# Block-sparse attention then token mix: the weight decoding kept out of the last two attention units, the first two mix steps' x turned earlier, and the block tables built after the first scores

## The chip, the cores and the metric

The kernel runs on one core of one Trainium2 chip. The metric is the device time of one launch in microseconds; a lower number is better. The engines are called as in the profile: PE is TensorE (PEld its weight loads), DVE VectorE, ACT ScalarE, POOL GpSimd, SP SyncE, whose queue issues nearly all DMAs.

## The reference

Two stages. The attention output of all heads is the token mix's input x. Everything is float32; the inputs of the mix weights are float64 words that the kernel decodes itself.

```python
def _attn_ref(q, k, v, sampled_blocks):            # B=4, H=8, S=768, D=64
    scores = scale * np.matmul(q, k.transpose(0, 1, 3, 2))
    # kept: blocks of 32 with |i - j| <= 1, first and last block row and column,
    # and 3 sampled key blocks for each query block
    scores = np.where(mask, scores, -1000000000.0)
    attn = np.exp(scores - np.max(scores, axis=-1, keepdims=True))
    attn = attn / (np.sum(attn, axis=-1, keepdims=True) + 1e-09)
    return np.matmul(attn, v)

def _moe_ref(x, w_theta, w_tok_r, w_tok_i, w_ch):  # x: 4 x 768 x 512
    theta = x @ w_theta
    zr, zi = x * np.cos(theta), x * np.sin(theta)
    y = np.einsum('ts,bsd->btd', w_tok_r, zr) + np.einsum('ts,bsd->btd', w_tok_i, zi)
    u = x + y
    return u + np.maximum(u @ w_ch, 0.0)
```

## The kernel before

**Attention** works on 52 units: for each of two pairs of batches, four wide units (the first and last query block against all 768 keys) and then 22 narrow units i = 1 to 22, one query block each. A unit passes through these steps: POOL copies the key blocks it needs into `kg` (L259) and gathers its sampled value rows into `vb` by an indirect DMA (L281); PE makes the scores `S` (L298, wide L386); DVE takes their extremes `m` (L301, wide L392); ACT takes exponentials into `P` (L310, wide L400); PE turns `P` into `T` (L316), and ACT copies that to `pT` (L318); PE multiplies by the values into `X` (L350) for two units at a time; DVE normalises into `xo` (L331 to L335), and SP writes `xo` to the DRAM buffer `xs` (L369). The steps of neighbouring units are interleaved by hand: the loop over n (L471 to L541) does the scores of unit n+1, the weights of n+1, the transposition of n, the values of earlier units, and the gathers of n+2. This stands in a `manual_schedule` block.

**Decoding.** The weights of theta and of the token mix are 22 pieces of 64-bit words. A piece takes a load by SP (L61, 512 KB), then three phases: `bits` (DVE L69 to L71, after ACT's `start` L65), `rest` (DVE L77, L79) and `low` (DVE L85, L86, after ACT's `high` L82). These 66 phases are dealt out over the units by `shares`: weight 0 for the first two units, 2 for a wide one, 1 for any other (L432 to L436). The loop gives each unit the phases that bring it up to its share: `decoder.ahead` does ACT's part, `decoder.go` DVE's part, and the low phase of a piece issues the load of the piece after next.

**Tables.** `Tables` loads the sampled block numbers and turns them into the row numbers that POOL's gathers use. `make` (L130 to L161) is nine small DVE operations on `sb_scratch` and `sb_block` and some on POOL; `rest` follows in unit 0.

**Token mix.** `follow` is a generator, resumed three times. Before its first `yield` it issues the loads of x for mix steps 0 and 1 from `xs`: `xr` (L585) for the transposed form, `xa` (L572) for the plain one, four DMAs each, in a pool whose room is that of the key tile `kb`, so it can begin when POOL's last copy from `kb` is done. Then it does `turn(0)` and `turn(1)` (DVE transposes to `r` L601, ACT's high part `xTh` L602, DVE's low part `xTl` L603; `r` has one buffer), loads ACT's Sin table (L689), and does `theta(0)` and `theta(1)` (PE L611 to L613, then a chain of ACT L615, L616 and DVE L618 to L620, ACT L622 to L624). `turned` multiplies by x and splits (L633 to L637), and `mix` (L649 to L651) accumulates `y` on PE, 24 matmuls for each of 48 steps. The four PSUM banks of `y` are those of attention's `T` and `X`, so the first `mix` waits for the last `xo`. At the end `out` multiplies by the channel weights (L672 to L674).

Before the change the loads of x are issued at the start of the unit before the last, and everything from `turn(0)` to `theta(1)` in the last unit, behind its transposition and its decoding (L533 to L535).

Of the kernel before, what the change touches and what calls it, by code (L numbers as in the profile page):

```python
# [88 lines left out]
class Decoder:  # L89
# [11 lines left out]
    def ahead(self, n):  # L101

        for k in range(self.at, min(self.at + n, 3 * len(self.pieces))):
            piece = self.pieces[k // 3]
            if k % 3 == 0:
                piece.start()
            elif k % 3 == 2:
                piece.high()

    def go(self, n):  # L110
        for k in range(self.at, min(self.at + n, 3 * len(self.pieces))):
            piece = self.pieces[k // 3]
            (piece.bits, piece.rest, piece.low)[k % 3]()
            if k % 3 == 2 and k // 3 + 2 < len(self.pieces):
                self.pieces[k // 3 + 2].load(self.pool, self.queue)
        self.at += n
# [64 lines left out]
def attention(tc, qT, qE, kT, vr, sampled, xs, ident, pieces, follow):  # L181
# [8 lines left out]
    nc = tc.nc  # L190
    with ExitStack() as ctx, ExitStack() as scored, ExitStack() as early:
# [8 lines left out]
        cp = ctx.enter_context(tc.tile_pool(name="acp", bufs=1))  # L200
# [30 lines left out]
        def load_k(bp, b, pp):  # L231
            if (b, pp) == (0, 0):
                kbs[bp] = kp.tile([P, 8, NB, 32], F32, tag="kb", name=f"kb{bp}")
            nc.sync.dma_start(kbs[bp][:, 4 * b + 2 * pp : 4 * b + 2 * pp + 2], kT[bp, b][:, 2 * pp : 2 * pp + 2])
# [5 lines left out]
        def load_edges(bp):  # L240
            qes[bp] = ep.tile([P, 2, 4, 64], F32, tag="qe", name=f"qe{bp}")
            nc.sync.dma_start(qes[bp].rearrange("r b p f -> r (b p f)"), qE[bp])

        def turn_edges(bp):
            t = qes[bp].rearrange("r b p f -> r (b p f)")
            nc.vector.tensor_scalar(t, t, -0.125, None, op0=ALU.mult)
# [126 lines left out]
        def load_v_wide(bp, b, pp):  # L373
            v = vp.tile([P, 6, 260], F32, tag="vw", name=f"vw{bp}_{b}_{pp}")
            c0 = 260 * (2 * b + pp)
            nc.sync.dma_start(v, vr[768 * bp : 768 * bp + 768, c0 : c0 + 260].rearrange("(c s) f -> s c f", s=P))
            vws[bp, b, pp] = v
# [51 lines left out]
        units = []  # L429
# [1 line left out]
            units += [(bp, "w", x) for x in WIDE] + [(bp, i, None) for i in range(1, NB - 1)]  # L431
        shares, total = [], 0.0  # L432
        for n in range(len(units)):
            weight = 0.0 if n < 2 else 2.0 if units[n][1] == "w" else 1.0
            total += weight
            shares.append(total)  # L436

        def do(n, inner, wide=None):

            if 0 <= n < len(units):  # L440
                bp, i, x = units[n]
                if i != "w":
                    inner(bp, i)
                elif wide:
                    wide(bp, *x)

        def is_wide(n):
            return 0 <= n < len(units) and units[n][1] == "w"

        def first_of_pair(n):  # L450
            return n < len(units) and units[n][1] == "w" and units[n][2] == (0, 0)
# [3 lines left out]
        with tc.manual_schedule():  # L455
            load_edges(0)
            load_k(0, 0, 0)
            tab = Tables(nc, wp, sampled)
            turn_edges(0)
            tab.make(nc, cp)  # L460
            load_k(0, 0, 1)
            load_v_wide(0, 0, 0)
            load_k(0, 1, 0)
            load_v_wide(0, 0, 1)
            load_k(0, 1, 1)
            for i in (1, 3):
                load_q(0, i)
            decoder = Decoder(pieces, stage, nc.sync)
            do(0, scores, scores_wide)
            do(0, weights, weights_wide)  # L470
            for n in range(len(units) + 1):  # L471
                if n == len(units) - 2:
                    early.close()
                    next(follow)
                phases = 0
                if n < len(units):
                    phases = round(shares[n] / total * 3 * len(pieces)) - decoder.at
                if n + 4 < len(units) and not is_wide(n + 4) and units[n + 4][:2] not in ((0, 1), (0, 3)):
                    load_q(*units[n + 4][:2])
                if first_of_pair(n + 10):  # L480
                    load_edges(1)
                for pp in range(2):
                    if first_of_pair(n + 16 - 6 * pp):
                        load_v_wide(1, 0, pp)
                do(n + 2, gather_k)
                if first_of_pair(n + 3):
                    for b, pp in WIDE:
                        load_k(1, b, pp)
                do(n + 3, number_blocks)
                do(n + 2, scale_q)  # L490
                if first_of_pair(n + 2):
                    turn_edges(1)
                decoder.ahead(phases)
                last = None
                if is_wide(n):
                    bp, _, x = units[n]
                    if n and not is_wide(n - 1):
                        last = units[n - 2][:2]
                        values(*last)
                    turn_wide(bp, *x, 0)  # L500
                    do(n + 1, scores, scores_wide)
                    if n and is_wide(n - 1):
                        values_wide(bp, *units[n - 1][2], 1)
                    do(n + 1, weights, weights_wide)
                    turn_wide(bp, *x, 1)
                    decoder.go(phases)
                    if n == 0:
                        tab.rest(nc)
                    if last:
                        finish(*last)  # L510
                    values_wide(bp, *x, 0)
                    if n and is_wide(n - 1):
                        finish_wide(bp, *units[n - 1][2])
                elif n == len(units):
                    last = units[n - 2][:2]
                    values(*last)
                    finish(*last)
                else:
                    bp, i, _ = units[n]
                    do(n + 1, scores, scores_wide)  # L520
                    if i == 1:
                        values_wide(bp, *units[n - 1][2], 1)
                    elif i % 2:
                        last = bp, i - 2
                        values(*last)
                    if i % 2:
                        do(n + 1, weights, weights_wide)
                        turn(bp, i)
                    else:
                        turn(bp, i)  # L530
                        do(n + 1, weights, weights_wide)
                    decoder.go(phases)
                    if n == len(units) - 1:  # L533
                        scored.close()
                        next(follow)  # L535
                    if last:
                        finish(*last)
                    if i == 1:
                        finish_wide(bp, *units[n - 1][2])
                do(n + 2, load_pair)  # L540
                do(n + 2, gather_v)  # L541
            assert not decoder.left(), decoder.left()


def token_mix(tc, w, ch_pieces, xs, outT, bias, nb):
# [7 lines left out]
    nc = tc.nc  # L553
    with ExitStack() as late, ExitStack() as ctx:
# [3 lines left out]
        half_pi, up_int, down_int, early = bias  # L558
# [3 lines left out]
        def at(k):  # L562
            return k // 12, (k // 6) % 2, k % 6
# [23 lines left out]
        def tok(b, j):  # L587
            return [t[:, :, 128 * (j % 3) : 128 * (j % 3) + 128] for t in xT[b, j // 3]]

        def turn(k):  # L590
            b, h, j = at(k)
            if h:
                return
            if j % 3 == 0:
                tp = tps[min((2 * b + j // 3) % 3, 1)]
                xT[b, j // 3] = [tp.tile([P, 4, 384], F32R, tag=f"xT{x}", name=f"xT{x}{b}_{j}") for x in "hl"]
            hi, lo = tok(b, j)
            raw = xr.pop((b, j))
            r = xp.tile([P, 4, 128], F32, tag="r", name=f"r{k}", bufs=1)
            for c in range(4):  # L600
                nc.vector.transpose(r[:, c, :].rearrange("p (i t) -> p i t", t=32), raw[:, :, c])  # L601
            nc.scalar.copy(hi, r)  # L602
            nc.vector.tensor_tensor(lo, r, hi.bitcast(F32), op=ALU.subtract)  # L603
# [77 lines left out]
        for k in range(2):  # L681
            load_raw(k, xp)
            load(k)
        yield
        ps_h = ctx.enter_context(tc.tile_pool(name="ps_h", bufs=3, space=PSUM, side="right"))
        ps_o = ctx.enter_context(tc.tile_pool(name="ps_o", bufs=1, space=PSUM, side="right"))
        turn(0)
        turn(1)
        nc.scalar.activation(early, half_pi, AF.Sin)  # L689
        theta(0)  # L690
        theta(1)
# [4 lines left out]
        cp = late.enter_context(tc.tile_pool(name="mcp", bufs=1))  # L696
# [117 lines left out]
```

## Time and profile before

| what | us |
|---|---|
| median of 3 runs | 617.61 (616.85 to 617.62) |
| the profiled execution's own time | 614.82 |
| span of its instructions | 613.0 |
| PE busy | 546.7 (89%) |
| DVE busy | 451.7 (74%) |
| ACT busy | 334.7 (55%) |
| POOL busy | 150.1 (24%) |

The span is counted from the first instruction to the last, and 1.8 us of the execution lie around it. All times of rows are microseconds from the start of the span, so a row tells at which place of the program it stands: attention runs to about 274 us, the token mix from there to the end. The columns of a timeline row are start, duration, engine, line, operation, destination<-sources, shapes, count, and in brackets how long the engine had been idle before it and what ended that. The columns of a windows row are the stretch, its length, then busy time and number of instructions of PE, PEld, DVE, ACT and POOL, the granted PE clock as a share of full speed, the DMA engines' busy share and GB/s.

### The profile page before, as it was taken

What the parts mean: (1) busy time and instruction counts of PE and PEld (TensorE: products, weight loads), DVE (VectorE), ACT (ScalarE), POOL (GpSimd) and SP (SyncE); (2) the same over time, 40 slices, a digit from 0 to 9 for tenths busy, and PEclk for the clock granted to TensorE, in tenths of its full rate; (3) what the DMA queues carried; (4) which work ended last, traced back from release to release, by engine and by line L of the source; (5) the groups of instructions that cost most, each with busy time, mean ns of one, the idle gap of its engine ahead of it and who ended that gap; (6) DMA issues with size and microseconds to landing.
All of it is one profiled execution on the core that took longest, in us unless ns stands there. A gap on an engine that the chain in (4) does not pass through costs nothing.

```text
span 613.0 us, 16813 instructions
## 1 busy us (share of the span) xinstructions
PE 546.7 (89%) x6636; PEld 482.5 (79%) x6636; DVE 451.7 (74%) x1063; ACT 334.7 (55%) x708; POOL 150.1 (24%) x262
## 2 busy tenths in 40 slices
PE   4869787866788898869999999999999999999997
PEld 1546565553565575559999999999999999999997
DVE  2798898854988989768999894846974748657554
ACT  2567767653665776655756563455542655433520
POOL 1457877604166888300000000000000000000000
PEclk9999999887998999878999999999999999999999
DMA  8788999785588988835531242211342111211002
GB/s 293 272 239 241 323 310 324 227 307 167 165 258 275 287 254 275 218 107 163 151 113 57 66 137 83 74 46 40 105 121 74 48 52 47 79 61 57 18 1 103
DMA packets 62686, 95.59 MB, mean 156 GB/s; under 512 B 9104, under 2 KB 44560, under 8 KB 62608
## 3 DMA queue, kind: packets, MB, share of 16 engines
q1 hardware_dynamic: 56272, 71.09, 38.3%
q0 software_dynamic: 6336, 23.43, 11.8%
q8 instruction: 52, 0.85, 0.6%
q14 instruction: 26, 0.21, 0.1%
HBM read 81.90 MB, written 12.58 MB: 154 GB/s over the span
## 4 chain that ended last, share of the span: by engine, by line
PE 66%; DVE 13%; ACT 8%; DMA 7%; issue 3%; SPq 2%; POOL 0%; POOLq 0%; DVEq 0%; ACTq 0%
PE y L649 9%; PE y L650 9%; PE y L651 9%; PE X L350 5%; PE S L298 4%; PE T L316 4%; PE o L674 4%; PE o L673 4%; PE o L672 4%; PE h L613 3%; PE h L612 3%; PE h L611 3%; DVE m L301 3%; ACT pT L318 2%; ACT P L310 2%
## 5 line engine op out<-in xcount | busy, mean ns | idle before, releaser
L259 POOL COPY kg<-kb 128x256 f32 (+2 forms) x202 | 103.3, 550 | 64.1 <-PE S L298 32.7
L310 ACT ACTIVATE P<-S,m 128x256 f32<-128x256 f32 x176 | 69.1, 479 | 30.1 <-DVE m L301 25.5
L649 PE MATMUL y<-w_tok_r_hi,zh 128*128 128x384 f32 x192 | 65.3, 340 | 4.0 <-DVE xo L335 3.7
L301 DVE TENSOR_REDUCE m<-S 128x2 f32<-128x512 f32 x88 | 56.3, 681 | 12.3 <-PE S L298 12.0
L650 PE MATMUL y<-w_tok_r_lo,zh 128*128 128x384 f32 x192 | 64.9, 338 | 0.0
L651 PE MATMUL y<-w_tok_r_hi,zl 128*128 128x384 f32 x192 | 64.9, 338 | 0.0
L649 PE MATMUL y<-w_tok_i_hi,zh 128*128 128x384 f32 x192 | 64.9, 338 | 0.0
L650 PE MATMUL y<-w_tok_i_lo,zh 128*128 128x384 f32 x192 | 64.8, 338 | 0.0
L316 PEld LDWEIGHTS T<-ident,P 128*128 128x128 f32 x352 | 39.6, 146 | 30.9 <-ACT pT L318 22.7
L316 PE MATMUL T<-ident,P 128*128 128x128 f32 x352 | 50.4, 288 | 14.7 <-ACT pT L318 13.5
L318 ACT COPY pT<-T 128x1024 f32<-128x1024 f32 x44 | 44.8, 1018 | 33.1 <-PE T L316 32.9
L651 PE MATMUL y<-w_tok_i_hi,zl 128*128 128x384 f32 x192 | 62.3, 338 | 0.0
L298 PE MATMUL S<-kg,q 64*32 64x256 f32 x1408 | 54.5, 406 | 7.0 <-issue 6.1
L611 PE MATMUL h<-w_theta_hi,xTh 128*128 128x256 f32 x192 | 54.7, 285 | 2.4 <-ACT xTh L602 2.4
L615 ACT ACTIVATE t<-h,up_int 128x256 f32<-128x256 f32 x48 | 22.8, 474 | 60.4 <-PE h L613 56.5
L613 PE MATMUL h<-w_theta_hi,xTl 128*128 128x256 f32 x192 | 54.6, 285 | 0.0
L612 PE MATMUL h<-w_theta_lo,xTh 128*128 128x256 f32 x192 | 54.4, 284 | 0.0
L281 POOL DMA_INDIRECT vb<-in_vr_dram,rows x44 | 44.9, 1019 | 35.6 <-PE X L350 28.4
L673 PE MATMUL o<-ul,w_ch_hi 128*128 128x384 f32 x128 | 42.9, 335 | 0.0
L674 PE MATMUL o<-uh,w_ch_lo 128*128 128x384 f32 x128 | 42.9, 335 | 0.0
L672 PE MATMUL o<-uh,w_ch_hi 128*128 128x384 f32 x128 | 42.4, 335 | 0.0
L649 PEld LDWEIGHTS y<-w_tok_r_hi,zh 128*128 128x128 f32 x192 | 36.7, 191 | 4.5 <-ACT cs L623 3.9
(129 smaller groups left out, 1248.8 us busy)
## 6 DMA issues: line engine op xcount, KB each, us to landing
xa<-xs SPq DMA_DIRECT2D x192, 64.0 KB, 2.0
vw<-in_vr_dram SPq DMA_DIRECT2D x8, 780.0 KB
kb<-in_kT_dram SPq DMA_DIRECT2D x8, 768.0 KB
xr<-xs SPq DMA_DIRECT2D x96, 64.0 KB, 2.0
out_dram<-of SPq DMA_DIRECT2D x32, 192.0 KB, 1.9
va<-in_vr_dram SPq DMA_DIRECT2D x22, 260.0 KB, 6.1
q<-in_qT_dram SPq DMA_DIRECT2D x22, 256.0 KB, 6.2
xs<-xo SPq DMA_DIRECT2D x88, 64.0 KB, 5.2
```

Source lines behind the costliest of these rows:

```text
L259: nc.gpsimd.tensor_copy(dst, blocks.rearrange("r g s f -> r s g f"))
L298: nc.tensor.matmul(sc[32 * p : 32 * p + 32, e, b, :], q[rows, b, p, :], keys[rows, :, :, place(b, p), :], start=True, stop=True)
L301: nc.vector.tensor_reduce(m[:, e], sc[:, e], axis=AX.X, op=ALU.min)
L310: nc.scalar.activation(pt[:, e, b, :], sc[:, e, b, :], AF.Exp, bias=m[:, e, b : b + 1], scale=-1.0)
L316: nc.tensor.transpose(t[:, k, :], pt, ident)
L611: nc.tensor.matmul(ps, hi[:, c, :], wh[:, c, :], start=c == 0, stop=False)
L612: nc.tensor.matmul(ps, hi[:, c, :], wl[:, c, :], start=False, stop=False)
L613: nc.tensor.matmul(ps, lo[:, c, :], wh[:, c, :], start=False, stop=c == 3)
L649: nc.tensor.matmul(acc, zh[:, dd], wh[:, j, tt], start=j == 0 and m == 0, stop=False)
L650: nc.tensor.matmul(acc, zh[:, dd], wl[:, j, tt], start=False, stop=False)
L651: nc.tensor.matmul(acc, zl[:, dd], wh[:, j, tt], start=False, stop=j == 5 and m == 1)
L673: nc.tensor.matmul(ps, wh[:, c, :], ul, start=False, stop=False)
```

## The change

There are four parts. The last two units get decoding weight 0, so the 66 phases are dealt out over a total weight of 54 instead of 56, and where a unit holds the first and third phase of one piece, `high` is issued between them. The loads of x for steps 0 and 1 are written at the end of the third unit from the end, behind POOL's last copy from `kb`. `turn(0)` and `turn(1)` stand in the last unit but one, and a new `yield` keeps the table load and the two theta steps back for the last unit, behind its transposition. `tab.make` is called after the first wide scores instead of before them.

```diff
@@ Decoder
-            elif k % 3 == 2:
+            elif k % 3 == 2 and k - 2 < self.at:
                 piece.high()
     def go(self, n):
             piece = self.pieces[k // 3]
+            if k % 3 == 2 and k - 2 >= self.at:
+                piece.high()
             (piece.bits, piece.rest, piece.low)[k % 3]()
@@ attention
-            weight = 0.0 if n < 2 else 2.0 if units[n][1] == "w" else 1.0
+            weight = 0.0 if n < 2 or n >= len(units) - 2 else 2.0 if units[n][1] == "w" else 1.0
...
             turn_edges(0)
-            tab.make(nc, cp)
             load_k(0, 0, 1)
...
             do(0, scores, scores_wide)
+            tab.make(nc, cp)
             do(0, weights, weights_wide)
             for n in range(len(units) + 1):
-                if n == len(units) - 2:
-                    early.close()
-                    next(follow)
...
                 do(n + 2, gather_k)
+                if n == len(units) - 3:
+                    early.close()
+                    next(follow)
...
                     decoder.go(phases)
-                    if n == len(units) - 1:
+                    if n == len(units) - 2:
+                        next(follow)
+                    elif n == len(units) - 1:
                         scored.close()
                         next(follow)
@@ token_mix
         yield
+        turn(0)
+        turn(1)
+        yield
         ps_h = ctx.enter_context(tc.tile_pool(name="ps_h", bufs=3, space=PSUM, side="right"))
         ps_o = ctx.enter_context(tc.tile_pool(name="ps_o", bufs=1, space=PSUM, side="right"))
-        turn(0)
-        turn(1)
         nc.scalar.activation(early, half_pi, AF.Sin)
```

Where this moves instructions is seen in the order of each engine's queue. The numbers behind names are those of buffers, and lines of the changed kernel stand two to five lower. First DVE at the start of the program, before the change:

```order
L246 TENSOR_SCALAR qe_126<-qe_126 128x512
L134 CAST sb_scratch<-sb_scratch 128x72
L136 TENSOR_SCALAR sb_scratch<-sb_scratch 128x72
L138 CAST sb_block<-sb_scratch 1x3x24
L155 TENSOR_TENSOR sb_scratch<-sb_scratch 128x72
...
L160 SCALAR_TENSOR_TENSOR sb_scratch<-sb_scratch 128x72
L392 TENSOR_REDUCE mw_00_179<-SW_000_169 128x1
L392 TENSOR_REDUCE mw_00_179<-SW_001_170 128x1
L392 TENSOR_REDUCE mw_01_204<-SW_010_194 128x1
```

And the same place after it:

```order
L248 TENSOR_SCALAR qe_126<-qe_126 128x512
L394 TENSOR_REDUCE mw_00_158<-SW_000_148 128x1
L394 TENSOR_REDUCE mw_00_158<-SW_001_149 128x1
L136 CAST sb_scratch<-sb_scratch 128x72
L138 TENSOR_SCALAR sb_scratch<-sb_scratch 128x72
L140 CAST sb_block<-sb_scratch 1x3x24
L157 TENSOR_TENSOR sb_scratch<-sb_scratch 128x72
...
L162 SCALAR_TENSOR_TENSOR sb_scratch<-sb_scratch 128x72
L394 TENSOR_REDUCE mw_01_204<-SW_010_194 128x1
```

The two reductions of the first wide unit now stand ahead of the nine table operations, and these stand ahead of the second unit's reductions.

Second, DVE at the end of attention, from the last narrow unit's reduction (`m_22`) on, before the change:

```order
L69 TENSOR_SCALAR da_tok_i_4274<-da_tok_i_4274 128x512
L70 TENSOR_SCALAR da_tok_i_4274<-da_tok_i_4274 128x512
L71 SCALAR_TENSOR_TENSOR da_tok_i_4274<-raw_tok_i_4091,da_tok_i_4274 128x512
L301 TENSOR_REDUCE m_22_4365<-S_22_4348 128x2 x2
L77 TENSOR_SCALAR ds_tok_i_4434<-da_tok_i_4274 128x512
L79 SCALAR_TENSOR_TENSOR raw_tok_i_4091<-raw_tok_i_4091,ds_tok_i_4434 128x512
...
L335 TENSOR_TENSOR xo_19_4440<-X_19_4368,sm_19_4437 128x512
L85 TENSOR_TENSOR da_tok_i_4274<-da_tok_i_4274,w_tok_i_hi 128x512
L86 TENSOR_TENSOR w_tok_i_lo<-da_tok_i_4274,raw_tok_i_4091 128x512
L601 STREAM_TRANSPOSE r_4468<-xr_0_4328 128x128 x4
L603 TENSOR_TENSOR xTl_0_4467<-r_4468,xTh_0_4466 128x4x128
```

And after it:

```order
L85 TENSOR_TENSOR da_tok_i_4124<-da_tok_i_4124,w_tok_i_hi 128x512
L86 TENSOR_TENSOR w_tok_i_lo<-da_tok_i_4124,raw_tok_i_3932 128x512
L303 TENSOR_REDUCE m_22_4371<-S_22_4354 128x2 x2
L605 STREAM_TRANSPOSE r_4442<-xr_0_4295 128x128 x4
L607 TENSOR_TENSOR xTl_0_4441<-r_4442,xTh_0_4440 128x4x128
L605 STREAM_TRANSPOSE r_4449<-xr_1_4305 128x128 x4
L607 TENSOR_TENSOR xTl_0_4441<-r_4449,xTh_0_4440 128x4x128
...
L337 TENSOR_TENSOR xo_19_4459<-X_19_4374,sm_19_4456 128x512
L622 SCALAR_TENSOR_TENSOR rr_4499<-t_4496,h_4483 128x256
```

The decoding of the last piece is gone from behind `m_22`, and both steps' transposes stand there, with the normalisation of `xo_19` behind them.

Third, ACT at the same place, before the change and after it:

```order
L318 COPY pT<-T_21_4424 128x32x32
L82 CAST w_tok_i_hi<-da_tok_i_4274 128x512
L318 COPY pT<-T_22_4447 128x32x32
L602 CAST xTh_0_4466<-r_4468 128x4x128
L602 CAST xTh_0_4466<-r_4475 128x4x128
L689 ACT_TABLE_LOAD
L689 ACTIVATE early<-half_pi 128x1
L615 ACTIVATE t_4496<-h_4483,up_int 128x256
```

```order
L320 COPY pT<-T_21_4430 128x32x32
L606 CAST xTh_0_4440<-r_4442 128x4x128
L606 CAST xTh_0_4440<-r_4449 128x4x128
L320 COPY pT<-T_22_4465 128x32x32
L694 ACT_TABLE_LOAD
L694 ACTIVATE early<-half_pi 128x1
L619 ACTIVATE t_4496<-h_4483,up_int 128x256
```

The copy of the last transposition, `T_22`, has changed places with the two `xTh` casts: it now stands behind the second of them and directly ahead of the table load. On SP the order of the x loads of steps 0 and 1 is the same in both kernels: behind the last `va` load come `xr_0`, `xa_0`, `xr_1` and `xa_1`, four DMAs each.

## The prediction

> **What bounds the kernel now.** I read the share of each engine in the chain first, then busy time by stage, then the waits where the two stages meet, and last the timelines of that place and of the start.
>
> The chain that ended last, by engine, from the page:
>
> ```profile
> PE 66%; DVE 13%; ACT 8%; DMA 7%; issue 3%; SPq 2%; POOL 0%; POOLq 0%; DVEq 0%; ACTq 0%
> ```
>
> By stage:
>
> ```profile
> 40.00:130.00 90.00, 73.17 (x1780) 51.62 (x1780) 75.99 (x141) 59.94 (x119) 59.99 (x100) 0.94 0.93 289
> 130.00:160.00 30.00, 20.69 (x299) 13.65 (x298) 16.46 (x25) 14.38 (x19) 7.44 (x14) 0.89 0.59 199
> 160.00:250.00 90.00, 75.47 (x1819) 53.27 (x1820) 79.55 (x148) 61.78 (x121) 67.44 (x109) 0.96 0.87 262
> 250.00:274.00 24.00, 15.83 (x278) 12.51 (x277) 16.19 (x39) 14.96 (x30) 0.70 (x1) 0.84 0.53 135
> 274.00:280.00 6.00, 6.00 (x19) 6.00 (x20) 3.78 (x13) 1.90 (x5) 0.00 (x0) 0.51 0.60 166
> 280.00:607.00 327.00, 326.70 (x2058) 326.38 (x2057) 233.61 (x635) 163.37 (x391) 0.00 (x0) 1.00 0.26 76
> ```
>
> From 280 to 607 PE is busy 326.7 of 327 us at full clock. The change does not touch that stage's work, so it can pay only by letting mix start earlier, or by giving mix's first 6 us (274 to 280, clock 0.51) a full clock. In attention no engine is full: between 40 and 130 and between 160 and 250 DVE is busy 76 and 80 us of 90, PE 73 and 75, and they alternate on the chain. The waits of PE between 240 and 285:
>
> ```profile
> PE y L649 <- DVE xo L335: 3.7, 1, 3.7
> PE h L611 <- ACT xTh L602: 2.4, 1, 2.4
> ```
>
> Both are at the handover. The first ends the stage; the second is in front of theta. I ask of each part what it does to the first.
>
> **Part 1, tables behind the first scores.** PE, DVE, PE, DVE at the start:
>
> ```profile
> 5.83 2.84 PE L386 MATMUL SW<-kb,qe 64*64 64x512 f32 x16 [5.83 <-DMA kb<-in_kT_dram]
> 7.51 0.28 DVE L134 CAST sb_scratch<-sb_scratch 128x72 f32<-128x72 int32 x1 [3.71 <-DMA sb_scratch<-in_sampled_dram]
> 9.40 0.23 DVE L160 SCALAR_TENSOR_TENSOR sb_scratch<-sb_scratch 128x72 f32<-128x72 f32 x1
> 9.55 1.81 DVE L392 TENSOR_REDUCE mw<-SW 128x1 f32<-128x768 f32 x2
> 15.91 0.96 DVE L392 TENSOR_REDUCE mw<-SW 128x1 f32<-128x768 f32 x1 [4.54 <-PE SW L386]
> 17.87 2.57 POOL L259 COPY kg<-kb 128x512 f32<-128x512 f32 x6 [15.00 <-DVE sb_scratch L168]
> ```
>
> The scores are there at 8.67, and the reduction starts at 9.55, behind the nine table operations. With 0.05 us for the handover (15.86 to 15.91 at the second unit) it starts at 8.72: **0.8 us** earlier, and the chain of exponential, transposition and second scores with it. The table operations, 7.51 to 9.6, 2.1 us, fall into DVE's idle 4.54 us before the second reduction; without that cover they would cost the 2.1 again. POOL first needs the block numbers at 17.87. Bounds: 0, if a transfer later takes the gain back, and -0.8. I take -0.8, since nothing in attention is tied to the clock on the wall but transfers that are issued by the same queues, and these move along.
>
> **Part 2, phases dealt out anew.** By `shares`, units 2 to 25 get 32 phases instead of 31, the four wide units 26 to 29 get 10 instead of 9, units 30 to 49 get 24 in both, and the last two 0 instead of 2. DVE's two operations of a low phase, mean over 40 to 250:
>
> ```profile
> L85 DVE TENSOR_TENSOR da_tok_r<-da_tok_r,w_tok_r_hi 128x512 f32<-128x512 f32 x8 | 7.8, 971 | 0.0
> L86 DVE TENSOR_TENSOR w_tok_r_lo<-da_tok_r,raw_tok_r 128x512 fp32r<-128x512 f32 x8 | 5.9, 742 | 0.3
> ```
>
> Such a phase is 0.971 + 0.742 = 1.7 us, and I price every phase so. Of the two added ones, the one in the wide units (about 130 to 160) I cost at nothing: DVE is busy only 16.5 of 30 us there; uncovered it costs 1.7. The other falls among units where DVE has some 30% of the chain (13% of 613 us are 80 us, nearly all of them before 274): 0.3 x 1.7 = **+0.5 us**. Bounds: both fully on the path, +3.4, and below nothing -1.8, since another order of DVE can spare or add one stall of PE's own queue such as this:
>
> ```profile
> 250.90 0.37 PE L298 MATMUL S<-kg,q 64*32 64x256 f32 x1 [1.78 <-issue]
> ```
>
> **Part 3, the handover.** ACT, then DVE, then SP, then PE, before the change:
>
> ```profile
> 258.50 1.01 ACT L318 COPY pT<-T 128x1024 f32<-128x1024 f32 x1 [0.16 <-PE T L316]
> 259.40 0.62 ACT L82 CAST w_tok_i_hi<-da_tok_i 128x512 fp32r<-128x512 f32 x1
> 260.75 1.01 ACT L318 COPY pT<-T 128x1024 f32<-128x1024 f32 x1 [0.72 <-PE T L316]
> 262.36 0.62 ACT L602 CAST xTh<-r 128x512 fp32r<-128x512 f32 x1 [0.60 <-DVE r L601]
> 264.66 0.62 ACT L602 CAST xTh<-r 128x512 fp32r<-128x512 f32 x1 [1.68 <-DVE r L601]
> 265.30 1.28 ACT L689 ACT_TABLE_LOAD   x1
> ...
> 260.06 0.69 DVE L85 TENSOR_TENSOR da_tok_i<-da_tok_i,w_tok_i_hi 128x512 f32<-128x512 f32 x1 [1.32 <-ACT w_tok_i_hi L82]
> 261.39 0.88 DVE L601 STREAM_TRANSPOSE r<-xr 128x128 f32<-128x128 f32 x4
> 263.74 0.89 DVE L601 STREAM_TRANSPOSE r<-xr 128x128 f32<-128x128 f32 x4
> 273.15 0.69 DVE L335 TENSOR_TENSOR xo<-X,sm 128x512 f32<-128x512 f32 x1
> ...
> 252.22 2.80 SPq L585 DMA_DIRECT2D xr<-xs  x4
> 259.19 1.85 SPq L585 DMA_DIRECT2D xr<-xs  x4
> 264.06 1.83 SPq L369 DMA_DIRECT2D xs<-xo  x4
> ...
> 273.99 0.66 PE L649 MATMUL y<-w_tok_r_hi,zh 128*128 128x384 f32 x1 [3.74 <-DVE xo L335]
> ```
>
> From the table load (265.30) to the first `y` (273.99) is 8.7 us of ACT and DVE in turn; their order is the same in both kernels from the load on, and `y` stands behind the last `xo`, which DVE holds back to 273.15. So mix moves as the table load moves. What DVE does for x no longer waits for decoding: the first transposes could go at 257 instead of 261.39, and theta(0) right behind the last transposition. But the second transposes need `xr_1`:
>
> ```profile
> DMA to landing us min/median/max: 1.9/2.0/2.1
> ```
>
> Its fourth DMA is issued at 259.19 + 3 x 0.47 = 260.6 and lands 2.0 later, at 262.6. From there: 0.97 to the cast (261.39 to 262.36), 0.64 for it (264.66 to 265.30), 0.9 for the copy of `T_22`, which now stands behind the casts (258.50 to 259.40): table load at 265.1, **0.2 us** earlier than now. The gain of the early turn is eaten by the wait for `xr_1`, with the copy queued behind it on ACT and the last `X` on PE behind that copy. PE's theta and `X` are ready long before 272.7 and cost nothing.
>
> What may bring `xr_1` forward is the transfers ahead of it: the last 512 KB of weights, now issued at about 241, goes three units earlier.
>
> ```profile
> 250.00:251.00 1.00, 0.10 (x1) 0.00 (x0) 0.00 (x0) 0.94 (x2) 0.70 (x1) 1.00 0.79 218
> ```
>
> At 262 GB/s (160 to 250) 512 KB are 2.0 us, the most it can give. But the DMA engines stood at 0.79 at 250, before the x loads began, so they had nearly caught up. I take -0.2, which makes this part **-0.4 us**; bounds -2.2 and +0.9, the copy on the path with nothing won. SP is moved past too: the write of `xo_19`, at 264.06 before, comes behind the loads of step 2 and needs an `xo` that is now behind the turns, ready at about 266. The DMA behind it waits for `turned(0)` in any case:
>
> ```profile
> SPq L572 <- DVE rr L633: 2.9, 1, 2.9
> ```
>
> So its 1.83 us of issue fit into a wait of 2.9; uncovered, `xr_2` would be 1.8 later.
>
> **The clock.** The granted clock (next to last but one number) falls to 0.50 in three stretches:
>
> ```profile
> 253.00:254.00 1.00, 1.00 (x21) 0.14 (x4) 0.97 (x3) 1.00 (x3) 0.00 (x0) 0.50 0.90 298
> 256.00:257.00 1.00, 1.00 (x41) 0.90 (x33) 0.98 (x3) 0.24 (x1) 0.00 (x0) 1.00 1.03 187
> ...
> 274.00:275.00 1.00, 1.00 (x3) 1.00 (x4) 0.50 (x3) 0.10 (x1) 0.00 (x0) 0.50 0.55 161
> 279.00:280.00 1.00, 1.00 (x5) 1.00 (x4) 0.41 (x3) 0.56 (x1) 0.00 (x0) 0.55 0.91 290
> ```
>
> The first lasts 3.2 us, mix's own 5.6 (273.99 to about 279.6) and costs half of that, 2.8. With theta and `X` done earlier, PE's idle time before `y` grows from 3.74 to about 6 us, so mix starts at half clock in any case; I leave the 2.8 as it is. [...]
>
> **The sum**: -0.8 + 0.5 - 0.4 = -0.7 us against the profiled 614.82, so 614.1 there. The median of the runs stands 2.8 above the profiled one; the same step from 617.61 gives **616.9**.
>
> **Rivals.**
> - *The transfers give way.* `xr_1` lands 2.0 earlier: part 3 is -2.2 and the sum -2.5, 615.1. For it: shares of 0.87 between 160 and 250. Against: the 0.79 at 250.
> [...]
> - *Slower: DVE on the path of attention pays for what it gave up at the end.* Both added phases in full, +3.4, give +2.2 with the rest, 619.8. It decides once the phases cost over 2.4, which is 1.2 more than the gains of parts 1 and 3 together. For it: DVE busy 88% of 160 to 250. Against: its 30% of the chain.
> - *The change does not do what it says.* The 0.8 is lost on the way to 250 and the load of `xr_1` holds ACT as now: 617.6.
>
> **How the numbers follow.** What a measurement of this kernel can tell from no change is about 0.2%, 1.2 us. Chances: forecast 0.46, transfers 0.20, clock 0.14, slower 0.13, nothing 0.07. Faster by over 1.2 us are the second and third and a part of the first: 0.38. Slower: 0.13 and a little of the first: 0.14. Within: 0.48. The forecast's own range is 615.6 to 618.2. The range over the cases: 614.2, the transfers with 0.9 more, to 619.0, where most of the slower case is left out.
>
> **What would show it.** Part 1: the first reduction at about 8.7 and the second transposition's scores 0.8 earlier. Part 2: the handover's `m_22` less than 0.8 earlier than before, apart from the 1.4 us of decoding ahead of it. Part 3: ACT waiting for DVE's `r` ahead of the second cast, the table load directly behind the copy, and 8.7 us from it to the first `y`; theta(0) some 2 us earlier with no gain behind it. Wrong it would be if the table load gained more than 1 us on what parts 1 and 2 leave it, if mix's first matmuls ran at full clock, or if PE waited for `xr_3` in the first steps of mix.

## The result, and the profile after

The changed kernel takes **619.59 us** (median of 20 runs, 614.64 to 628.08), the kernel before, run beside it, 615.26 (20 runs, 609.57 to 622.57). The ratio is **1.0069, 95% interval 1.0044 to 1.0093**: 4.3 us slower, between 2.7 and 5.7. The forecast was 0.7 us faster; its range, moved by the same 2.35 us as the median of before (617.61 to 615.26), ends at 616.7. Both miss the result. The ratios here and below leave out executions over 1.5% above the fastest of their kernel, among them one of x3 of 1779.65 us and one of before of 1035.89; the medians are of all. The profiled execution of the changed kernel took 621.24, its span is 619.1.

The chain of the changed kernel by engine, from its page:

```profile
PE 64%; DVE 16%; ACT 7%; DMA 7%; issue 4%; SPq 2%; ACTq 0%; DVEq 0%
```

Its waits of PE between 240 and 300 (who waited for whom, us in total, times, longest):

```profile
PE y L653 <- DVE xo L337: 4.9, 1, 4.9
...
PE y L653 <- ACT zh L640: 3.2, 1, 3.2
PE h L615 <- ACT xTh L606: 1.4, 1, 1.4
```

Its windows in mix, columns as before:

```profile
290.00:293.00 3.00, 3.00 (x28) 3.00 (x27) 2.13 (x7) 0.06 (x1) 0.00 (x0) 1.00 0.70 190
293.00:297.00 4.00, 0.76 (x5) 0.56 (x4) 3.68 (x14) 4.00 (x12) 0.00 (x0) 0.94 0.52 153
297.00:300.00 3.00, 3.00 (x11) 3.00 (x11) 3.00 (x12) 2.80 (x8) 0.00 (x0) 0.51 0.52 142
```

The second wait is new, and it lies where the prediction saw nothing to lose: **in mix, behind its second step**. PE is full until 293.4, stands for 3.2 us until `zh` of step 2 is there, and then works at half clock (0.51) for another 3.3, to 299.9.

The first waits and the handover are much as forecast. DVE's first reduction of the changed kernel:

```profile
8.59 1.82 DVE L394 TENSOR_REDUCE mw<-SW 128x1 f32<-128x768 f32 x2 [4.64 <-PE SW L388]
```

ACT and PE at its handover:

```profile
261.49 1.01 ACT L320 COPY pT<-T 128x1024 f32<-128x1024 f32 x1 [1.46 <-PE T L318]
262.40 0.62 ACT L606 CAST xTh<-r 128x512 fp32r<-128x512 f32 x1
266.01 0.62 ACT L606 CAST xTh<-r 128x512 fp32r<-128x512 f32 x1 [2.98 <-DVE r L605]
266.53 1.01 ACT L320 COPY pT<-T 128x1024 f32<-128x1024 f32 x1
267.56 1.28 ACT L694 ACT_TABLE_LOAD   x1
...
276.25 0.66 PE L653 MATMUL y<-w_tok_r_hi,zh 128*128 128x384 f32 x1 [4.87 <-DVE xo L337]
```

From the table load to the first `y` it is 8.7 us, as before. But this all stands some 2 us later than before (273.99), so something was lost in attention too.

### The profile page after: what moved, and what is told of

The parts are those of the page before. It is cut to its first block, busy times and chain, and to the rows that moved or that the text cites. A ratio compares the mean times of both kernels' runs of the same rounds, so it can differ in the third digit from the quotient of the medians.

```text
span 619.1 us, 16816 instructions
## 1 busy us (share of the span) xinstructions
PE 548.1 (89%) x6636; PEld 484.5 (78%) x6636; DVE 450.6 (73%) x1063; ACT 332.7 (54%) x708; POOL 150.9 (24%) x262
## 4 chain that ended last, share of the span: by engine, by line
PE 64%; DVE 16%; ACT 7%; DMA 7%; issue 4%; SPq 2%; ACTq 0%; DVEq 0%
PE y L653 11%; PE y L654 10%; PE y L655 10%; DVE m L303 4%; PE o L678 4%; PE o L676 4%; PE o L677 4%; PE h L617 3%; PE h L616 3%; PE h L615 3%; PE S L300 3%; PE X L352 3%; PE T L318 3%; ACT P L312 2%; PE SW L388 2%
## 5 line engine op out<-in xcount | busy, mean ns | idle before, releaser
L318 PE MATMUL T<-ident,P 128*128 128x128 f32 x352 | 51.3, 291 | 19.9 <-ACT pT L320 17.5
L615 PE MATMUL h<-w_theta_hi,xTh 128*128 128x256 f32 x192 | 54.0, 281 | 1.4 <-ACT xTh L606 1.4
L619 ACT ACTIVATE t<-h,up_int 128x256 f32<-128x256 f32 x48 | 22.7, 473 | 57.8 <-PE h L617 56.0
```

What stands on the lines that cost most here:

```text
L318: nc.tensor.transpose(t[:, k, :], pt, ident)
L615: nc.tensor.matmul(ps, hi[:, c, :], wh[:, c, :], start=c == 0, stop=False)
```

## The search for the cause

**Where ACT and DVE stood.** An engine's rows stand in the order of their starts. L65 starts the decoding of a piece of channel weights. L615 (L619 in the changed kernel) is ACT's first step of theta(2), L620 (L624) the last step of DVE's part, and L622 (L626) the first step of ACT's Sin chain behind it. ACT, then DVE, in the kernel before:

```profile
282.37 0.48 ACT L615 ACTIVATE t<-h,up_int 128x256 f32<-128x256 f32 x1 [0.95 <-PE h L613]
...
287.34 0.41 ACT L622 ACTIVATE cs<-rr 128x256 f32<-128x256 f32 x1
...
290.82 0.43 ACT L65 ACTIVATE da_ch<-raw_ch 128x256 f32<-128x256 f32 x1 [0.24 <-DMA raw_ch<-in_w_ch_dram]
291.16 0.39 ACT L636 CAST zh<-cs 128x256 fp32r<-128x256 f32 x1
...
286.70 0.25 DVE L620 TENSOR_SCALAR rr<-rr 128x256 f32<-128x256 f32 x1
```

And in the changed kernel:

```profile
285.39 0.62 ACT L606 CAST xTh<-r 128x512 fp32r<-128x512 f32 x1 [1.56 <-DVE r L605]
...
286.23 0.47 ACT L619 ACTIVATE t<-h,up_int 128x256 f32<-128x256 f32 x1
...
288.31 0.62 ACT L606 CAST xTh<-r 128x512 fp32r<-128x512 f32 x1
292.94 0.43 ACT L65 ACTIVATE da_ch<-raw_ch 128x256 f32<-128x256 f32 x1 [4.01 <-DMA raw_ch<-in_w_ch_dram]
293.28 0.71 ACT L626 ACTIVATE cs<-rr 128x256 f32<-128x256 f32 x2
...
296.16 0.41 ACT L640 CAST zh<-cs 128x256 fp32r<-128x256 f32 x1
...
291.64 0.49 DVE L624 TENSOR_SCALAR rr<-rr 128x256 f32<-128x256 f32 x2
```

The diff has no line there. Mix is not in the `manual_schedule` block; its instructions are put in order by a planner from modelled times, and with other work ahead of mix it put L65 in front of the Sin chain. L65's input is a transfer. In the kernel before the same L65 waited 0.24 us, with the casts of `zh` directly behind it.

In the changed kernel ACT waited 4.0 us for `raw_ch`, with theta(2) behind it. But L65 held theta(2) only for the last 1.4 us of that, because DVE's part of theta(2) was done only at 291.9 (the first of the two L624 in that row; the other is theta(3)'s). The rest of the delay came earlier. ACT's first step of theta(2) starts 10.0 us behind the first `y` instead of 8.4, behind a cast of `xTh` that waited for DVE, and DVE's last step starts at 15.4 instead of 12.7, among DVE's own steps of decoding.

So theory A: the whole loss is this stall and its half clock. Rivals: B, attention pays for the phases of decoding that part 2 moved into it; C, the handover of part 3. Expectations of the first runs call L65 an exponential; it is the absolute value with which decoding begins.

### The parts alone, and the order alone

x1 is before with `tab.make` moved; x2 before with the two zero weights (and the guard for `high`); x3 before with the loads, turns and `yield` of part 3; x4 the changed kernel with

```diff
-                nc.scalar.copy(zh, f)
+                casts[k] = nc.scalar.copy(zh, f)
...
-                decoder.ahead(2)
+                if k == 4:
+                    with tc.issue_after(casts[2].ins):
+                        decoder.ahead(2)
+                else:
+                    decoder.ahead(2)
```

> The kernel before with part 1 alone (tables behind the first scores). Theory A (the loss of 4.3 us is a stall of PE in the second mix step: ACT's exponential of the decoder of the channel weights, L65, waits for its transfer with the Sin chain of theta(2) queued behind it, 3.2 us, and the half clock behind the stall, some 1.5 us): here that exponential stands behind step 2's chain as before, so no stall over 1 us between 285 and 300, and the time is that of before less the 0.8 us forecast for this part: 0 to -1.0 us. Rival B (attention pays for the two added phases of decoding): the same here, since the shares are untouched. Rival C (the handover itself): the same. A loss of over 1.2 us would be against all three.

> The kernel before with part 2 alone (no decoding in the last two units, the phases dealt out anew). Theory A: step 2's Sin stands ahead of the exponential of L65 on ACT, so the stall of 3.2 us behind zh does not appear in that form; the time is before +0 to +1.5 us (0.5 forecast for the phase on the path, and some of the wait may fall on the second casts of zh, which still stand behind one exponential). Rival B: the whole loss is here, +3 to +5 us, with m_22 late and no PE wait over 1 us between 285 and 300. Rival C: no loss.

> The kernel before with part 3 alone (loads of x earlier, x turned in the last unit but one, theta behind the last transposition; tables and shares as before). Theory A: the exponential of L65 stands ahead of step 2's chain on ACT, as in the changed kernel; PE waits 2.5 to 3.5 us for zh in the second mix step, a stretch of half clock follows, and the time is before +3 to +5 us. Rival B: no loss beyond 1 us, since decoding is dealt out as before. Rival C: the loss is here too, but between m_22 and the first y (over 18.9 us, as long as it took before), not in the second mix step.

> The changed kernel, with one order added: the next decoding of weights in mix is issued on ACT behind the second casts of zh of step 2. Theory A: the stall of 3.2 us and the half clock behind it are gone, PE runs through from the first y at full clock once it is lifted, and the time is 4 to 5 us below the changed kernel, that is before +0.3 to -1.0 us. Rival B and rival C: the stall is a symptom of one execution or is made up for later; the time stays that of the changed kernel, before +3 to +5 us.

| run | median (runs) | ratio, 95% interval | first y | first y to last matmul |
|---|---|---|---|---|
| before | 615.26 (20) | 1 | 273.99 | 335.2 |
| changed | 619.59 (20) | 1.0069 (1.0044 to 1.0093) | 276.25 | 339.0 |
| x1 part 1 | 615.72 (12) | 0.9984 (0.9948 to 1.0019) | 270.16 | 337.1 |
| x2 part 2 | 617.33 (12) | 1.0032 (0.9993 to 1.0070) | 273.32 | 338.1 |
| x3 part 3 | 617.84 (12) | 1.0034 (0.9996 to 1.0072) | 272.21 | 336.0 |
| x4 order | 616.73 (12) | 1.0037 (1.0001 to 1.0074) | 279.07 | 335.5 |

The medians of before in the groups of runs that follow are 615.8 to 617.5; the ratios are to the runs of the same group. By the medians no part alone carries the loss, though the intervals of x2 and x3 reach up to 1.0070 and 1.0072.

x4 took 3.5 us off mix. With L65 out of the way ACT waits for DVE instead:

```profile
294.70 0.72 ACT L626 ACTIVATE cs<-rr 128x256 f32<-128x256 f32 x2 [3.03 <-DVE rr L624]
```

The cast of `zh_2` comes 18.5 us behind the first `y` instead of 19.9, PE stands for 1.7 us instead of 3.2, and no second stretch at half clock follows. Off the time it took only about half of the loss (1.0037; the interval leaves 0.1 to 4.6 us): **theory A holds for mix and falls as the whole story**.

The order came with part 3. x3 has L65 ahead of the Sin chain too, x1 and x2 do not:

```profile
287.83 0.44 ACT L65 ACTIVATE da_ch<-raw_ch 128x256 f32<-128x256 f32 x1 [2.92 <-DMA raw_ch<-in_w_ch_dram]
```

So theory A was right on the order in x3, and wrong on its cost: PE stood for 1.7 us there, no half clock followed, mix took 336.0, and the time is 2.1 us above before (-0.2 to 4.4) where 3 to 5 were expected. x2's own stall was another one: its first L65 waited 4.1 us, with the turn of x behind it.

### Mix cut off, and the decoding moved out of mix's start

y1 and y2 are before and changed, ended behind the second mix step. In y3 (changed) and y4 (before) nothing of the decoding can stand ahead of `zh_2`:

```diff
-            if 0 < k < 13:
-                decoder.ahead(2)
-                decoder.go(2)
+            if 2 < k < 11:
+                with tc.issue_after(casts[2].ins):
+                    decoder.ahead(3)
+                decoder.go(3)
```

> The kernel before, cut off behind the second mix step: steps 2 to 47 of mix, the channel product and most of the output are left out (four tiles of the partial sums of y are written out instead). It ends some 15 us behind the first y, so at about 292 us, and is the base for the next run. In mix itself all six profiles so far fit one sum: from the first y to the last matmul 331.9 us, plus PE's stalls, plus half of the time at half clock (before 335.2 of which 0.3 stall and 5.6 at half clock, changed kernel 339.0 with 3.2 and 7).

> The changed kernel, cut off at the same place. Theory A (the loss arises in the second mix step and behind it): within 1.5 us of the cut kernel before, 0.7 below it if the prediction's sum holds. Rival B (attention pays for the two phases of decoding) and rival C (handover): the whole 4.3 us, at least 3 us, are already here.

> The changed kernel with the decoding of the channel weights in mix begun at step 3 (three phases a step instead of two from step 1) and its activations issued on ACT behind the second casts of zh of step 3's predecessor, so that nothing of that decoding stands ahead of zh_2 on ACT. Theory A: no PE stall over 0.5 us between the first y and 310, one stretch of half clock at the start only, the time from first y to the last matmul is 333.5 to 334.5 instead of 339.0, and the kernel is 4 us or more below the changed kernel: 0.3 to 1.5 us under before. Rivals B and C: at best 2 us below the changed kernel, still above before by 2.

> The kernel before with the same order of decoding in mix. All theories: not slower than before. Theory A: before pays less for these waits (0.3 us in its one profile, 2.8 in that of the tables alone, which has the same order), so it gains 0 to 2.5 us, and the two kernels with this order differ by the prediction's -0.7, within 1.5. Rivals B and C: the changed kernel stays 4 above this one.

The cut kernels took 294.12 and 299.5 (6 runs each, 290.5 to 298.9 and 290.6 to 300.9): too wide to settle anything, but on the side of a loss ahead of mix. y3 took 615.07, y4 **612.23** (ratio 0.9946, 0.9898 to 0.9994). ACT of y3 (its PE's only wait in mix up to 330 stands below it):

```profile
287.40 0.42 ACT L626 ACTIVATE cs<-rr 128x256 f32<-128x256 f32 x1 [0.55 <-DVE rr L624]
...
288.88 0.39 ACT L640 CAST zh<-cs 128x256 fp32r<-128x256 f32 x1
...
290.19 0.75 ACT L65 ACTIVATE da_ch<-raw_ch 128x256 f32<-128x256 f32 x2
```

PE's wait of y3:

```profile
PE y L653 <- ACT zh L640: 1.3, 1, 1.3
```

From the first `y` to the cast of `zh_2` it is 14.6 us here, 19.9 in the changed kernel, 17.2 before. By the ratios the later decoding took 4.4 us off the changed kernel and 3.3 off before. So **both** paid for these waits, and the changed kernel still lies 3.1 us above before (six runs of each). Of that, 1.5 us are in mix (335.0 against 333.5, with the wait of 1.3 shown above). The rest should have been lost ahead of mix; these two profiles, with the first `y` at 274.25 and 274.75, do not show it.

### Part 2 without part 3, and another deal of the phases

The copies of `T` date every unit. In the first ten profiles those with part 2 lost 2.6 to 5.6 us on before between units 41 and 48, so theory D: the phases that part 2 puts there cost it. In z1 the last piece goes to the wide units 26 to 29, three phases each, and units 30 to 48 do what they did before:

```diff
-            weight = 0.0 if n < 2 or n >= len(units) - 2 else 2.0 if units[n][1] == "w" else 1.0
+            weight = 0.0 if n < 2 else 2.0 if units[n][1] == "w" else 1.0
...
+        ends = [round(x / total * 3 * len(pieces)) for x in shares]
+        ends = [min(e + (0 if n < 26 else (1, 2, 2, 3)[min(n - 26, 3)]), 3 * len(pieces)) for n, e in enumerate(ends)]
...
-                    phases = round(shares[n] / total * 3 * len(pieces)) - decoder.at
+                    phases = ends[n] - decoder.at
```

z2 is z1 with the later decoding; z3 parts 1 and 3 with it, z4 part 1 with it; n3 parts 1 and 2 with it, n4 part 1 and the other deal with it.

> The changed kernel with the phases dealt out otherwise: the last three phases (a whole piece of weights) go to the four wide units of the second pair (3 each instead of 2, 2, 3, 2), so that units 30 to 48 do the same phases as in the kernel before, unit 49 one, and the last two none. Theory D (new, from the last copies of T in ten profiles: between units 41 and 48 the five with part 2 lose 2.6 to 5.6 us on the kernel before, the five without it at most 1.3 either way; the new deal puts other phases, and the double one of unit 49, into these units, where DVE is 7.2 to 7.8 of 8 us busy): this loss goes, the wide units take the piece in DVE's idle time, and the time is 3 to 5 us under the changed kernel, that is before +1 to -1. Rival A (the stall in mix alone): no gain over 1 us, since mix is untouched. Rival C (the handover): no gain either.

> The same, with the later decoding in mix that gained some 4 us on both kernels (run y3 and y4). Theory D: 3 us or more under run y3 (the changed kernel with that mix, 615.1), so 610 to 612, at or below run y4 (612.2). Rivals A and C: as y3, 614 to 616.

> Parts 1 and 3 of the change without part 2, with that later decoding in mix. Theory D: part 2 alone costs, so this is 2.5 to 4 us under y3 and within 1 of y4 or below it (611 to 612.5). Rival C (the handover is what lost): as y3, 614 to 616.

> Part 1 alone with that later decoding in mix: 0.8 us under y4 by the prediction's term for the tables, 611 to 612. If it is under z3 by over 1.5 us, part 3 costs that.

n1 and n2 test something else, whether part 3 is bound by the landing of `xr_1` (theory E): both loads of `xr` are issued ahead of those of `xa`.

```diff
         for k in range(2):
             load_raw(k, xp)
+        for k in range(2):
             load(k)
```

> The changed kernel with one change: the loads of xr_0 and xr_1 are issued ahead of those of xa_0 and xa_1. Theory E (in part 3 the first y is bound by the landing of xr_1: 11.2 us behind it in the profile of the changed kernel): xr_1 is issued 3 us earlier on SP, DVE waits less than 0.5 us for it ahead of the second transposition, the table load comes 1 to 2 us earlier behind the last copy of T, and the time is 1 to 2 us under the changed kernel, 618. Rival (the copy of T_22 and theta bind, not the load): no difference over 0.5 us.

> Run z2 (the other deal of phases and the later decoding in mix) with xr_0 and xr_1 ahead of xa_0. Theory E: 2 us under z2 (615.8 mean), about 613.5, since here attention ends earlier and the load stands further in front (DVE waited 1.5 us for it, the copy of T_22 8 us after that of T_21). Rival: as z2.

> Parts 1 and 2 without part 3, with the later decoding in mix. Theory D (the phases that part 2 puts into units 41 to 48 cost some 4 us there, of which the empty last two units give back 1 to 1.5): 2 to 3 us above z4 (tables alone, 612.7 mean), 615. Rival C (part 3 is what costs): within 1 of z4.

> The same with the other deal (three phases in each wide unit of the second pair, units 30 to 48 as before, none in the last two) in place of that of part 2. Theory D: 2 to 4 us under n3, at z4 less up to 1.5: 611 to 612.5. Rival C: within 1 of n3.

| run, with the later decoding in mix | median (runs) | ratio, 95% interval | first y to last matmul |
|---|---|---|---|
| y4 before | 612.23 (6) | 0.9946 (0.9898 to 0.9994) | 333.5 |
| z4 part 1 | 612.27 (12) | 0.9965 (0.9929 to 1.0001) | 333.3 |
| z3 parts 1, 3 | 614.17 (12) | 0.9954 (0.9912 to 0.9996) | 333.5 |
| n3 parts 1, 2 | 616.18 (13) | 1.0005 (0.9971 to 1.0040) | 336.9 (an execution of 624.38) |
| y3 parts 1, 2, 3 | 615.07 (6) | 0.9997 (0.9954 to 1.0041) | 335.0 |
| n4 part 1, other deal | 617.40 (12) | 1.0000 (0.9961 to 1.0039) | 334.4 |
| z2 parts 1, 3, other deal | 616.23 (12) | 1.0014 (0.9981 to 1.0047) | 335.0 |
| n2 as z2, xr first | 614.94 (12) | 0.9953 (0.9915 to 0.9992) | 335.0 |
| *without it:* z1 | 620.84 (6) | 1.0113 (1.0079 to 1.0147) | 339.4 |
| *without it:* n1 changed, xr first | 618.18 (12) | 1.0030 (0.9997 to 1.0063) | 339.2 |

The medians without part 2 or the other deal are 612.2 to 614.2, those with one of them 614.9 to 617.4: with the decoding out of the way, part 2 costs and part 3 hardly does. n2's ratio, 0.9953, does not fit this; its median does. But the other deal is no better than part 2's own (n4 and n3, z2 and y3): **theory D falls** for the time. In the traces its loss between units 41 and 48 did go (-0.5 to +0.5 us in the four profiles of the other deal), and the time did not follow. What the two deals have in common is an added phase in the wide units, which the prediction had cost at nothing.

Theory E: SP issued `xr_1` behind `xr_0`, at 253.5 to 260.1 together. n1's table load came 5.5 us behind the copy of `T_21` instead of 6.1, a gain of 0.6 where 1 to 2 were expected. Its median is 1.4 below the changed kernel, n2's 1.3 below z2 (by the ratios 2.4 and 3.8), no more than the spread of runs allows.

### The queue of SP in the wide units

From the copy of the last unit of the first pair (133.99 in before) to that of the third narrow unit of the second (181.54), six profiles without part 2 and the other deal take 45.7 to 48.1 us, mean 47.1; five with part 2 **49.6 to 52.3, mean 50.8**; four with the other deal 49.3 to 52.1 (n3's execution of 624.38 us and the cut kernels are not among them). SP's timeline there in the kernel before:

```profile
146.34 0.33 SPq L61 DMA_DIRECT2D raw_tok_r<-in_w_tok_r_dram  x1
147.34 1.72 SPq L369 DMA_DIRECT2D xs<-xo  x4
154.28 0.40 SPq L376 DMA_DIRECT2D vw<-in_vr_dram  x1
154.72 0.54 SPq L223 DMA_DIRECT2D q<-in_qT_dram  x1
162.40 0.34 SPq L61 DMA_DIRECT2D raw_tok_i<-in_w_tok_i_dram  x1
```

And in the changed kernel:

```profile
147.97 1.73 SPq L371 DMA_DIRECT2D xs<-xo  x4
157.88 0.35 SPq L61 DMA_DIRECT2D raw_tok_i<-in_w_tok_i_dram  x1
158.33 0.40 SPq L378 DMA_DIRECT2D vw<-in_vr_dram  x1
158.77 0.53 SPq L225 DMA_DIRECT2D q<-in_qT_dram  x1
```

With part 2, unit 27 ends a piece (its phases are `rest, low, bits` instead of `bits, rest`). A low phase issues the load of the piece after next, and SP holds that load until DVE's L86 has freed its buffer, at 157.8. `vw`, the values of the next wide unit, free since about 154, is behind it (before it was issued at 154.28). The DMA engines of the changed kernel stand still meanwhile (its window, the share is the last but one number), and PE waits for `vw` (its timeline):

```profile
152.00:158.00 6.00, 4.86 (x78) 3.23 (x70) 4.33 (x7) 2.48 (x3) 0.00 (x0) 0.90 0.01 3
```

```profile
163.82 1.57 PE L415 MATMUL Xw<-vw,pT 128*64 128x65 f32 x24 [2.21 <-DMA vw<-in_vr_dram]
```

Their share is 0.01 there; before it was 0.40. In the five profiles with part 2 PE waits 2.3 to 3.8 us for `vw` in the wide units, in before 1.2. Theory F: this is what part 2 costs. In the other deal unit 27 has the same three phases and `vw` is late too, but PE does not wait for it there, so theory F leaves the length of those four stretches open. q1 issues `vw` ahead of the unit's decoding and changes nothing else; q2 adds `xr` first and the later decoding.

```diff
         def finish_wide(bp, b, pp):
-            if b == 0:
-                load_v_wide(bp, 1, pp)
...
                     turn_wide(bp, *x, 1)
+                    if n and is_wide(n - 1) and units[n - 1][2][0] == 0:
+                        load_v_wide(bp, 1, units[n - 1][2][1])
                     decoder.go(phases)
```

> The changed kernel with one change: in the wide units vw is loaded ahead of the decoding, so that on SP it stands ahead of the load of the next piece of weights, which waits for DVE. Theory F (part 2 costs by that queue: 3.8 us in the wide units): SP issues vw_1_0 at about 153 instead of 158.3 us, PE's wait for vw of 2.2 us is gone, the wide units take 2 to 3.8 us less (from the copy of the last unit of the first pair to that of the first narrow unit of the second, 41.2 to 44.2 us in the kernels with these shares, as against 40.7 in before), and the time is 1.5 to 3.5 us under the changed kernel (619.8 mean): 616.3 to 618.3. Rival D (the phases themselves cost, DVE's time): no gain over 0.5 us.

> The changed kernel with vw ahead, xr_0 and xr_1 ahead of xa_0, and the later decoding in mix (y3: 615.5 mean). Theory F with theory E: 615.5 less 1.5 to 3.5 and less 0.4 to 1.5, so 610.5 to 613.5, about as the tables alone with that decoding (z4, 612.7) or below it. Rival D: 614 to 615.

SP's timeline of q1, then its window:

```profile
147.71 1.72 SPq L371 DMA_DIRECT2D xs<-xo  x4
154.18 0.40 SPq L378 DMA_DIRECT2D vw<-in_vr_dram  x1
157.62 0.35 SPq L61 DMA_DIRECT2D raw_tok_i<-in_w_tok_i_dram  x1
```

```profile
152.00:158.00 6.00, 4.86 (x76) 3.29 (x72) 4.55 (x8) 2.47 (x3) 0.00 (x0) 0.93 0.42 126
```

The same stretch takes 46.8 us in q1 and 47.8 in q2, as without part 2, and PE's wait for `vw` is gone: for the wide units the mechanism is shown. The time of q1 did not follow: 619.59 (1.0064, 1.0030 to 1.0099), as the changed kernel. Its `y` comes 1.6 us earlier (274.67), but its stall in mix is 3.6 us and mix takes 339.4. **q2 takes 612.09, ratio 0.9948 (0.9909 to 0.9986)**, 3.0 under y3. How much of this is `vw` is not shown: `xr` first alone gave 1.3 and 1.4 by the medians and 2.4 and 3.8 by the ratios, and no run has `vw` ahead with the later decoding alone. q2's PE waits 0.2 us between the first `y` and 330:

```profile
PE y L653 <- ACT zh L640: 0.2, 1, 0.2
```

So q2 is faster than before and than the changed kernel. It is level with y4, the kernel before with the later decoding alone: the three parts, mended, have no gain that these runs can show.

## Why the prediction was wrong, point by point

- **"The change does not touch that stage's work": the step that failed first.** The work is the same, its order is not. L65 stands ahead of the Sin chain on ACT in the changed kernel, n1, q1 and z1, waits 3.8 to 4.0 us in all four, and mix takes 339.0, 339.2, 339.4 and 339.4 us from the first `y`. With before's order it takes 335.2 and 337.1 (before, x1). That is **+3 us**. In the two profiled executions the stall makes 2.9 of it (3.2 instead of 0.3) and the second stretch at half clock 1.7, and the shorter first stretch gives 1.4 back. L65's wait alone is not the stall: x4, without it, still stands for 1.7 us. The prediction had compared the two orders up to the first `y` only, and had taken a full PE at full clock behind it as proof that nothing can be lost there. It named the sign, PE waiting in the first steps of mix, but with another cause (`xr_3`).
- **Part 2, +0.5: the second.** "The one in the wide units I cost at nothing", since DVE idles there. A phase is not only DVE's 1.7 us: a low phase also issues a load, and this one was moved past `vw`. **+3.7 us** in the wide units (50.8 against 47.1). `m_22` came at 257.66 instead of 255.96. At the first `y` the five profiles with part 2 stand at 272.9 to 279.1, mean 275.2, the six without it and the other deal at 270.2 to 274.8, mean 272.8: about 2 us of the 3.7 arrive. The upper bound, +3.4, held that size by accident. The range used it only in a rival with a chance of 0.13.
- **The rival "slower, 619.8"** has the measured time by luck, with another mechanism. In the wide units DVE's time for the phases was not it: in q1 the phases are where they were, and the wide units are fast. Whether it costs between units 41 and 48 is not settled: there q1 and q2 still lose 4.7 and 4.4 us on before.
- **Part 1, -0.8: right.** The first reduction is at 8.59 instead of 9.55. The first narrow copy of `T` comes at 41.5 (mean of 13 profiles with part 1) instead of 42.9 (4 without). In the time of x1 it can't be told from nothing.
- **Part 3, -0.4: right on the waits at the handover, but not a gain.** ACT waits for `r`, the second cast and the copy of `T_22` stand directly ahead of the table load, and that comes 6.1 us behind the copy of `T_21` (6.8 before, y3 6.8, x4 6.6). The early theta(0) won nothing. Where attention ended earlier the load of `xr_1` set a floor: 7.7 to 9.0 us in x3, z1, z2 and z3. And it is with this part that the order of mix changed.
- **The clock.** Mix did start at half clock, for 3.2 us (276.25 to 279.4). Before it was 5.9 (273.99 to 279.9), where the prediction read 5.6. So the stretch was 2.7 shorter, the case "clock" of the chances (0.14), in this one execution, and its gain of 1.4 (an estimate, half of 2.7) went unseen under the stall. What sets the length of this stretch no run shows: by one profile each it is 3.2 us here, 5.3 in q2 and 5.9 in before. The one at 253 in before, read as 3.2, lasts 3.4 in the trace. The second cold stretch was not foreseen.
- **The sum.** +3 in mix and +2 at the first `y` make 5, beside a measured 4.3 (2.7 to 5.7). This is put together from single profiles; no run mends both and nothing else.

What stays open: why q1's earlier `y` is not seen in its time beyond the longer stall; why the wide units are as slow with the other deal; and where the 3.5 to 4.6 us that kernels with part 2 win in units 32 to 41 and the 0.9 to 4.9 that they lose in 41 to 50 come from.

## What to carry to other kernels

When a change moves work ahead of a stage that a planner orders by modelled times, compare the order of that stage too, engine by engine, down to the point where the queues agree again: in the changed kernel L65 on ACT waited 4.0 us for `raw_ch`, and theta(2) behind it, ready at 291.9, began at 293.28. A piece of decoding is priced with everything that it issues: DVE's idle time in the wide units did not hide the load of the low phase there, which SP held until 157.8 for its buffer, and `vw` behind it was issued at 158.33 instead of 154.28. And a stage that is full in one profile need not be full in the next: with the same order PE waited 0.3 us in mix in before and 2.9 in x1. Ask how late its next input comes.

## What the runs showed of the hardware

- Gaps of PE of 3.0 to 3.6 us in mix (changed, n1, z1, q1) were each followed by some 3.4 us at half clock; single gaps of up to 1.7 us (y3, x3, x4) left it at 1.00, and two of 1.3 us within 4 us in x2 were followed by 3.4 us at half clock (0.9 and 0.8 within 3.4 us in x1 were not). Half of 3.4 us is 1.7: by this estimate the gaps of 3.0 to 3.6 us cost about half as much again.
- Executions of one kernel spread by 13 us here (before: 609.6 to 622.6). Mix repeats more closely, by one profile of each kernel: 339.0 to 339.4 in four, 334.8 to 335.0 in y3, z2, n2 and q2, 333.3 to 333.5 in y4, z4 and z3, but 335.2 and 337.1 with before's own order. So most of the spread seems to lie ahead of it. Equal times of mix can be different sums: y3 has a wait of 1.3 us and 3.5 us at half clock, q2 a wait of 0.2 and 5.3. A single profile can date a wait but not weigh a change.
